# Attention over a small state in front of a two-layer MLP on one core: the second softmax's weights turned by a trip through DRAM and VectorE's 32x32 transposes in place of TensorE, and the first batch's order written anew

## The chip, the cores and the metric

The kernel runs on one core of one Trainium2 chip. The metric is device microseconds of one execution, from start to end. Five engines take part, each with its own queue of instructions: TensorE (PE in the profile; its weight loads are listed apart as PEld), VectorE (DVE), ScalarE (ACT), GpSimd (POOL) and SyncE (SP), which only issues DMAs here.

## The reference

For each of 8 batches and 8 heads, `x` holds 512 tokens of 64 numbers and `state` 32 rows of 64 numbers. Two softmaxes run over the same scores, one over the states, one over the tokens. Their results are put side by side (512 + 32 rows for each batch) and go through a two-layer MLP with 2048 hidden units and a smooth clipped activation.

```
scores  = scale * x @ state^T            # 512 x 32 for each batch and head
a       = softmax(scores, over states)
xread   = a @ state
scores2 = scale * state @ x^T            # 32 x 512
a2      = softmax(scores2, over tokens)  # the second softmax
sread   = a2 @ x
rows    = concat([xread, sread])         # 544 rows for each batch, 8 heads beside each other
h       = rows @ w_in                    # 512 -> 2048
g       = h if h >= 1, 0 if h <= -1, else (h + 1)^2 / 4
out     = g @ w_out                      # 2048 -> 512
```

## The kernel before, in words

**Two algebraic steps shape the work.** `xread` is never formed: `state` is multiplied into `w_in` first (tiles `sw`, line 393, 256 hidden columns to a piece), and the first softmax's weights (`ath` and `atl`, the high and the low part of a value, since each product is made of three reduced-precision ones) go straight against that product (lines 446 to 448, tile `h`). The second product (lines 504 to 506, tile `acc`) is made of three in the same way, from `gh`, `gl` and the two halves of `wo`. `sread` of all batches is collected in `srT` and goes through the MLP at the very end as a ninth, half-sized batch.

**The loop.** Hidden units are taken in eight steps j of 256. In each step of each batch TensorE makes `h` (12 products of 128x512), ScalarE and VectorE make the activation (`relu` L455, `square` L458, `bound` L462) and split it (`gh` L468, `gl` L473), and TensorE multiplies the step before with `w_out` (24 products). The attention of batch b + 1 is spread over the steps of batch b. In step 0 stand its scores (`sc`, L230), the first transposes, the maximum `top2` (L294) and the exponential `exp2` (L298, which also sums). In step 2 stands the rest of the first softmax. The sum over tokens `sread` (`read2`, L327) is made in step 0 of the batch after.

**The turn of the second softmax.** `scores2` lies with (head pair, state) on the 128 partitions and the 512 tokens along the free dimension, in two halves q (even and odd heads). `read2` contracts over tokens, so the exponentials have to lie with tokens on the partitions. `turn2` does that with eight 128x128 TensorE transposes into a PSUM tile `e2p` (L309), and `keep_turned` copies them back to SBUF on ScalarE (L313) and makes the reciprocals of the sums on VectorE (L315, L316).

**What sets the order.** The first batch is issued by hand. Its operations are numbered as they are declared, and the table `ORDER` lists them as words like `186P` (operation 186 on TensorE; S, A and D are SyncE, ScalarE and VectorE). The class `Plan` gives each operation an estimated time, and between TensorE operations that the plan sets apart it emits dummy matmuls (`warmed`, L175), which keep TensorE busy. While the first batch runs, the weights of the MLP are fetched in 16 pieces of 1 MB and turned into fp32: `high` (L558, ScalarE), `low` (L545 on VectorE or L550 on ScalarE, chosen by the table), `join` (L566, VectorE, which makes `w` or `wf`); for `w_out` then two parts (L573 ScalarE, L577 VectorE, tile `wo`). The joined `wf`, the first softmax's `zt` and batch 0's exponentials share two buffers with the tag `tmp`. From batch 1 on a list scheduler orders the instructions.

Of the kernel before, what the change touches and what calls it, by code (L numbers as in the profile page):

```python
# [8 lines left out]
F32 = mybir.dt.float32  # L9
# [3 lines left out]
AF = mybir.ActivationFunctionType  # L13
# [4 lines left out]
WARM = 10  # L18
PAD = 120
ORDER = (  # L20
# [12 lines left out]
)  # L33


class Plan:
# [52 lines left out]
    def emit(self, fill, first, until):  # L89

        self.times(ORDER)
        begun, done = self.begun, self.done
        idle = 0.0
        for k in sorted(begun, key=lambda k: begun[k]):
            if self.ops[k][0] == "PE":
                if begun[first] < begun[k] < begun[until]:
                    n = int((begun[k] - idle) / 0.34)
                    if n > 0:
                        fill(n)
                idle = done[k]  # L100
            run = self.ops[k][2]
            if "/" in self.ops[k][0]:
                run(self.where[k])
            else:
                run()
# [3 lines left out]
def state_exchange_moe(  # L109
# [35 lines left out]
    ps = ctx.enter_context(tc.tile_pool(name="ps", bufs=2, space=PSUM))  # L145
    wop = ctx.enter_context(tc.tile_pool(name="wop", bufs=NJ))
    rawp = ctx.enter_context(tc.tile_pool(name="rawp", bufs=2))

    def ps_acc(name):
        return ps.tile([P, DM], F32, tag="acc", bufs=4, name=name)  # L150
# [10 lines left out]
    def ps_mm(name):  # L161
        return ps.tile([P, 2, 512], F32, tag="mm", bufs=1, name=name)
# [39 lines left out]
    class Attention:  # L202
# [83 lines left out]
        def top2(self, q):  # L286
            b = self.b
            if q == 0:
                tag = "tmp" if b == 0 else "e2"
                self.e2 = work.tile([P, 2, S], F32, tag=tag, bufs=2 if b == 0 else 1, name=f"e2_{b}")  # L290
                self.nm2 = small.tile([P, 2], F32, tag="nm2", name=f"nm2_{b}")
                self.sum2 = small.tile([P, 2], F32, tag="sum2", name=f"sum2_{b}")
            nm = self.nm2[:, q:q + 1]
            nc.vector.tensor_reduce(out=nm, in_=self.sc[q], op=ALU.max, axis=AX.X, negate=True)  # L294
            nc.vector.tensor_scalar_mul(nm, nm, SCALE)

        def exp2(self, q):
            nc.scalar.activation(  # L298
                out=self.e2[:, q], in_=self.sc[q], func=AF.Exp, bias=self.nm2[:, q:q + 1],
                scale=SCALE, accum_out=self.sum2[:, q:q + 1],  # L300
            )

        def turn2(self):
            b, e2 = self.b, self.e2
            e2p = self.e2p = ps_mm(f"e2p{b}")
            for q in range(2):
                for t in range(NT):
                    cols = slice(t * P, (t + 1) * P)
                    nc.tensor.transpose(out=e2p[:, q, cols], in_=e2[:, q, cols], identity=ident)  # L309

        def keep_turned(self):
            b = self.b
            nc.scalar.copy(out=self.e2, in_=self.e2p)  # L313
            self.r2 = small.tile([P, 2], F32, tag="r2", name=f"r2_{b}")
            nc.vector.tensor_scalar_add(self.r2, self.sum2, 1e-9)  # L315
            nc.vector.reciprocal(out=self.r2, in_=self.r2)  # L316

        def read2(self):
            b = self.b
            xn = loaded.pop(("xn", b))  # L320
            sr = banks[1].tile([P, 512], F32, tag="h", name=f"sr{b}") if b else ps_mm(f"sr{b}")[:, 0]
            sr = self.sr = sr[:, :2 * D].rearrange("p (q d) -> p q d", q=2)
            for q in range(2):
                for t in range(NT):
                    for pr in range(NPR):
                        c0 = t * P + pr * NS
                        nc.tensor.matmul(  # L327
                            sr[pr * NS:(pr + 1) * NS, q], lhsT=self.e2[:, q, c0:c0 + NS],
                            rhs=xn[:, t, 2 * pr + q], start=t == 0, stop=t == NT - 1,
                        )  # L330

        def scale2(self):
# [17 lines left out]
        def second(self):  # L350
            for q in range(2):
                self.turn(q)
            for q in range(2):
                self.top2(q)
            for q in range(2):
                self.exp2(q)

        def first(self):
            for f in (self.top1, self.less1, self.exp1, self.sum1):
                for q in range(2):  # L360
                    f(q)
            self.inv1()
            for q in range(2):
                self.norm1(q)
            self.turn2()
            self.keep_turned()

        def halves(self):
            for q in range(2):
# [273 lines left out]
    def att_ops2(b):  # L643
# [3 lines left out]
        for q in range(2):  # L647
# [1 line left out]
            take = [("tmp" if b == 0 else "e2", ("e2", b))] if q == 0 else []  # L649
            op(("top2",) + k, "DVE", 0.8, m("top2", q), [("sc", b) if b else ("sc", b, 1)] + [("top2", b, 0)] * q, take=take)  # L650
            op(("exp2",) + k, "ACT", 0.66, m("exp2", q), [("top2",) + k], ends=[("sc", b)])
        op(("kept", b), "ACT", 0.95, m("keep_turned"), [("e2p", b)], ends=[("e2p", b)])
        if b == 0:
            op(("rs", b), "DVE", 0.25, m("scale2"), [("sr", b)], ends=[("sr", b)])
            op(("srT", b), "ACT", 0.3, m("keep"), [("rt", b)], ends=[("rt", b)])

# [73 lines left out]
    for side in range(2):  # L730
# [12 lines left out]
        2: lambda: tensor(("sc", 1), 1.22, lambda: att_start(1), [("dma", "sb", 1), ("dma", "xt", 1)],  # L743
                          take=[("mm", ("sc", 1))], ends=[("xt", 1)]),
        3: lambda: tensor(("rt", 0), 0.15, lambda: atts[0].keep2(), [("rs", 0)], take=[("mm", ("rt", 0))]),
        4: lambda: tensor(("e2p", 1), 0.92, lambda: atts[1].turn2(), [("exp2", 1, 0), ("exp2", 1, 1)],
                          take=[("mm", ("e2p", 1))]),
    }
    more = {0: [(0, 2)], 1: [(0, 3), (0, 4)], 3: [(0, 5), (0, 6)], 5: [(0, 7), (1, 0)]}
    for j in range(NJ):  # L750
# [84 lines left out]
def _laid_out(x, state, moe_w_in, moe_w_out):  # L835
# [2 lines left out]
    NS = state.shape[2]  # L838
    DM, FF = moe_w_in.shape
    return {  # L840
        "x": x.reshape(B, H, S // 128, 128, D).transpose(0, 3, 2, 1, 4),
        "xt": x.reshape(B, H // 2, 2, 2, S // 2, D).transpose(0, 3, 2, 5, 1, 4).reshape(B, 2, 128, H // 2, S // 2),
        "state": state.reshape(B, H // 2, 2, NS, D).transpose(2, 4, 0, 1, 3).reshape(128, B, H // 2, NS),
        "moe_w_in": moe_w_in.reshape(DM // 128, 128, FF // 256, 256).transpose(2, 1, 0, 3).reshape(FF // 256, 128, -1),
# [27 lines left out]
```

## Time and profile before

| | us |
|---|---|
| median of 3 runs | 654.04 (653.77 to 654.39) |
| the profiled execution | 653.93 |
| its span, first to last instruction | 651.9 |
| TensorE busy in the span | 642.5 |
| ScalarE busy | 362.3 |
| VectorE busy | 338.1 |
| one batch in the middle (two `read2` apart) | 72.5 |

The time of an execution is 2.0 us longer than the span, for what lies around the first and the last instruction. Busy time of TensorE is modelled at the end of each matmul, so two starts that follow each other tell more than a duration: in the middle of the kernel one 128x512 matmul starts 0.23 us after another, though each is listed with 0.39 us.

### The profile page before, as it was taken

The numbers are of one execution on the slowest core, as the hardware profiler recorded it, in microseconds if no ns is written. First come the engines' busy times: TensorE is split into PE (matmuls) and PEld (weight loads), VectorE is DVE, ScalarE is ACT, GpSimd is POOL, SyncE is SP. The second block draws the span as 40 slices with busy tenths as digits, with TensorE's granted clock in tenths as the row PEclk, the third lists the DMA queues.
The fourth block names the chain that finished last, engine by engine and source line by source line (L and its number), as shares of the span: only waits on it lengthen the run. The fifth ranks groups of instructions, "written<-read, shape, count | busy, mean of one in ns | idle before, by whom it ended". The sixth has DMA issues, their size and how long they took to land.

```text
span 651.9 us, 10329 instructions
## 1 busy us (share of the span) xinstructions
PE 642.5 (99%) x4438; PEld 521.2 (80%) x4438; DVE 338.1 (52%) x484; ACT 362.3 (56%) x474; POOL 0.8 (0%) x7
## 2 busy tenths in 40 slices
PE   7999999999999999999999999999999999999997
PEld 6777887878787887878787887878787878788895
DVE  5999958533584338443574339343663334334431
ACT  5999766554565456454664457444664464444632
POOL 0000000000000000000000000000000000000000
PEclk9999999999999999999999999999999999999999
DMA  8996005000400004000500014000300010000101
GB/s 347 387 401 253 1 10 185 0 1 2 168 27 1 1 32 163 0 2 2 193 2 1 1 46 149 1 2 1 130 1 1 0 67 1 0 2 1 64 1 33
DMA packets 11085, 43.64 MB, mean 67 GB/s; under 512 B 1312, under 2 KB 1440, under 8 KB 7968
## 3 DMA queue, kind: packets, MB, share of 16 engines
q1 hardware_dynamic: 6096, 34.28, 13.6%
q10 hardware_dynamic: 4944, 8.72, 3.6%
q8 instruction: 34, 0.56, 0.4%
q14 instruction: 11, 0.09, 0.0%
HBM read 34.08 MB, written 8.91 MB: 66 GB/s over the span
## 4 chain that ended last, share of the span: by engine, by line
PE 96%; DVE 2%; ACT 1%; DMA 0%; issue 0%; POOL 0%; SPq 0%; DVEq 0%; POOLq 0%
PE acc L504 19%; PE acc L505 19%; PE acc L506 19%; PE h L446 10%; PE h L447 10%; PE h L448 10%; PE sw L393 5%; PE sc L230 1%; PE warmed L175 1%; PE sr L327 1%; PE e2p L309 1%; DVE w L566 0%; DVE u L462 0%; DMA out_dram<-o 0%; DVE z L237 0%; DVE z L252 0%
## 5 line engine op out<-in xcount | busy, mean ns | idle before, releaser
L504 PE MATMUL acc<-wo,gh 128*128 128x512 f32 x544 | 214.0, 393 | 0.0
L505 PE MATMUL acc<-wo,gh 128*128 128x512 f32 x544 | 212.1, 390 | 0.0
L506 PE MATMUL acc<-wo,gl 128*128 128x512 f32 x544 | 211.9, 390 | 0.0
L455 ACT ACTIVATE u<-h,half 128x512 f32<-128x512 f32 (+1 forms) x128 | 91.7, 717 | 178.3 <-PE h L448 170.2
L462 DVE SCALAR_TENSOR_TENSOR u<-u,h 128x512 f32<-128x512 f32 (+1 forms) x128 | 86.4, 714 | 199.8 <-ACT u L458 199.6
L504 PEld LDWEIGHTS acc<-wo,gh 128*128 128x128 f32 x544 | 102.2, 188 | 24.4 <-issue 3.3
L506 PEld LDWEIGHTS acc<-wo,gl 128*128 128x128 f32 x544 | 102.1, 188 | 21.6
L505 PEld LDWEIGHTS acc<-wo,gh 128*128 128x128 f32 x544 | 102.2, 188 | 20.6 <-DVE wo L577 0.2
L473 DVE TENSOR_TENSOR gl<-u,gh 128x1024 fp32r<-128x1024 f32 x68 | 83.2, 1224 | 56.5 <-ACT gh L468 56.5
L468 ACT CAST gh<-u 128x1024 fp32r<-128x1024 f32 x68 | 71.5, 1052 | 66.0 <-DVE u L462 63.4
L458 ACT ACTIVATE u<-u 128x1024 f32<-128x1024 f32 x68 | 72.1, 1061 | 1.8
L393 PE MATMUL sw<-w,sb 64*32 64x256 f32 x1024 | 32.3, 380 | 2.5 <-DVE w L566 2.5
L393 PEld LDWEIGHTS sw<-w,sb 64*32 64x32 f32 x1024 | 18.2, 106 | 11.9 <-DVE u L462 2.5
L519 ACT COPY o<-acc 128x512 f32<-128x512 f32 x33 | 19.0, 583 | 12.1 <-PE acc L506 12.1
L446 PE MATMUL h<-ath,sw_3h 128*128 128x512 f32 x64 | 25.1, 393 | 0.0
L446 PE MATMUL h<-ath,sw_5h 128*128 128x512 f32 x64 | 25.0, 391 | 0.0
L447 PE MATMUL h<-ath,sw_5l 128*128 128x512 f32 x64 | 24.9, 389 | 0.0
L448 PE MATMUL h<-atl,sw_5h 128*128 128x512 f32 x64 | 24.9, 389 | 0.0
L447 PE MATMUL h<-ath,sw_3l 128*128 128x512 f32 x64 | 24.9, 389 | 0.0
L448 PE MATMUL h<-atl,sw_3h 128*128 128x512 f32 x64 | 24.9, 389 | 0.0
L446 PE MATMUL h<-ath,sw_1h 128*128 128x512 f32 x60 | 24.4, 407 | 0.5 <-DVE u L462 0.5
L447 PE MATMUL h<-ath,sw_1l 128*128 128x512 f32 x60 | 23.4, 391 | 0.0
(158 smaller groups left out, 722.5 us busy)
## 6 DMA issues: line engine op xcount, KB each, us to landing
xt<-in_xt_dram SPq DMA_DIRECT2D x16, 512.0 KB, 5.2
raw_i<-in_moe_w_in_dram SPq DMA_DIRECT2D x8, 1024.0 KB, 7.0
raw_o<-in_moe_w_out_dram SPq DMA_DIRECT2D x8, 1024.0 KB, 11.4
xn<-in_x_dram SPq DMA_DIRECT2D x8, 1024.0 KB, 6.1
out_dram<-o ACTq DMA_DIRECT2D x32, 256.0 KB, 2.0
sb<-in_state_dram SPq DMA_DIRECT2D x1, 448.0 KB, 8.5
out_dram<-o SPq DMA_DIRECT2D x4, 64.0 KB, 1.7
out_dram<-o ACTq DMA_DIRECT2D x4, 64.0 KB, 2.0
```

What stands on the lines that cost most here:

```text
L393: nc.tensor.matmul(banks[hh][pr * NS:(pr + 1) * NS, cols], lhsT=sb[rows, b, pr], rhs=w32[c][rows, pr], start=True, stop=True,)
L446: nc.tensor.matmul(o, lhsT=wh[:, k, sl], rhs=ah[:, k], start=first, stop=False)
L447: nc.tensor.matmul(o, lhsT=wl[:, k, sl], rhs=ah[:, k], start=False, stop=False)
L448: nc.tensor.matmul(o, lhsT=wh[:, k, sl], rhs=al[:, k], start=False, stop=last)
L455: nc.scalar.activation(out=u, in_=h, func=AF.Relu, scale=0.5, bias=half)
L458: nc.scalar.activation(out=self.u, in_=self.u, func=AF.Square)
L462: nc.vector.scalar_tensor_tensor(out=u, in0=u, scalar=1.0, in1=h, op0=ALU.min, op1=ALU.max)
L468: nc.scalar.copy(out=gh, in_=self.u)
L473: nc.vector.tensor_tensor(out=gl, in0=self.u, in1=gh.bitcast(F32), op=ALU.subtract)
L504: nc.tensor.matmul(a, lhsT=lh, rhs=oh, start=f == 0, stop=False)
L505: nc.tensor.matmul(a, lhsT=lh, rhs=ol, start=False, stop=False)
L506: nc.tensor.matmul(a, lhsT=ll, rhs=oh, start=False, stop=f == NF - 1)
```

## The change

For batches 1 to 7 the turn is made in another way. `exp2` writes the exponentials so that a quarter t of the tokens (128 of them) of both halves q lies together. `trade` writes that tile to DRAM with one DMA (512 KB) and reads it back with four, so that partition block t of 32 holds quarter t for all four head pairs r; that exchanges blocks of 32 partitions with blocks of the free dimension. `turn_traded` then transposes each 32x32 block with one VectorE instruction over 1024 elements of each partition, and makes the reciprocals as before. The eight TensorE transposes and the ScalarE copy of these batches are gone. `read2` takes its weights through a view `turned`, and the host lays `x` out so that the tokens stand on the partitions in the new order (the same 1 MB for each batch).

Batch 0 keeps TensorE's transposes; there `exp2` writes its output in another order of columns, so that the turned tile has the same order of tokens. Its table `ORDER` is another one throughout. Operations are now emitted in the order of the table itself and not sorted by planned start.

```diff
 ORDER = (
-    "0S 87P 86A 1S 2S 88P 6S 97D 90D 89P 91D 99D 92D 10S 93D 100D 94D 3A 98D 101D 95A 33S 102A 96D "
...
+    "86A 0S 87P 1S 88P 2S 3A 90D 97D 91D 98D 89P 99D 92D 100D 93D 101D 10S 4D 6S 94D 102A 95A 5D "
...
+    "175A 176D 238P 239P 179A 234A 235D 236A 180D 237D 85D 59S "
...
-        for k in sorted(begun, key=lambda k: begun[k]):
+        for k in begun:
...
+    dram = ctx.enter_context(tc.tile_pool(name="dram", bufs=2, space=bass.MemoryType.DRAM))
...
         def exp2(self, q):
+            if self.b:
+                o, i = self.e2[:, :, q], self.sc[q].rearrange("p (t k) -> p t k", k=P)
+            else:
+                o = self.e2.rearrange("p t q k -> p (t q k)")
+                o = o[:, q * S:(q + 1) * S].rearrange("p (j t i) -> p t j i", j=NT, i=NS)
+                i = self.sc[q].rearrange("p (t j i) -> p t j i", j=NT, i=NS)
             nc.scalar.activation(
-                out=self.e2[:, q], in_=self.sc[q], func=AF.Exp, bias=self.nm2[:, q:q + 1],
-                scale=SCALE, accum_out=self.sum2[:, q:q + 1],
+                out=o, in_=i, func=AF.Exp,
+                bias=self.nm2[:, q:q + 1], scale=SCALE, accum_out=self.sum2[:, q:q + 1],
             )
...
+        def trade(self):
+            self.e2x = work.tile([P, NPR, 2 * P], F32, tag="tmp", name=f"e2x{self.b}")
+            there = dram.tile([P, NT, 2 * P], F32, tag="e2d", name=f"e2d{self.b}")
+            nc.sync.dma_start(out=there, in_=self.e2.rearrange("p t q k -> p t (q k)"))
+            for t in range(NT):
+                nc.sync.dma_start(
+                    out=self.e2x[t * NS:(t + 1) * NS], in_=there[:, t].rearrange("(r n) k -> n r k", n=NS)
+                )
+
+        def turn_traded(self):
+            e2 = self.e2.rearrange("p t q k -> p (t q k)")
+            nc.vector.transpose(out=e2, in_=self.e2x.rearrange("p r k -> p (r k)"))
+            self.turned = e2.rearrange("p (r q j n) -> p r q j n", q=2, r=NPR, n=NS)
+            self.inv2()
...
         def second(self):
...
             for q in range(2):
                 self.exp2(q)
+            self.trade()
...
         def first(self):
...
-            self.turn2()
-            self.keep_turned()
+            self.turn_traded()
...
-        op(("kept", b), "ACT", 0.95, m("keep_turned"), [("e2p", b)], ends=[("e2p", b)])
-        if b == 0:
+        if b:
+            op(("trade", b), "SP", 6.5, m("trade"), [("exp2", b, 0), ("exp2", b, 1)], take=[("tmp", ("e2x", b))])
+            op(("kept", b), "DVE", 1.3, m("turn_traded"), [("trade", b)], ends=[("e2x", b)])
+        else:
+            op(("kept", b), "ACT", 0.95, m("keep_turned"), [("e2p", b)], ends=[("e2p", b)])
...
-        4: lambda: tensor(("e2p", 1), 0.92, lambda: atts[1].turn2(), [("exp2", 1, 0), ("exp2", 1, 1)],
-                          take=[("mm", ("e2p", 1))]),
```

**What moves, first place: the start of batch 0 on ScalarE and TensorE.** ScalarE before, around the activation of the first hidden step (`u_0` is its tile, `raw_i_200` the third piece of `w_in`, `sw_1` the product of `state` with the second piece):

```order
L407 CAST sw_1h<-sw_1_234 128x2x256
L558 ACTIVATE raw_i_200<-raw_i_200 128x1024
L455 ACTIVATE u_0_220<-h_0_221,half 128x1024
L458 ACTIVATE u_0_220<-u_0_220 128x1024
L298 ACTIVATE e_0_247,sum_0_249<-sc_0_119,nm_0_248 128x512
```

ScalarE in the changed kernel, the same place (the third piece is `raw_i_202` there):

```order
L586 ACTIVATE raw_i_202<-raw_i_202 128x1024
L578 ACTIVATE raw_i_202<-raw_i_202,offset 128x1024
L483 ACTIVATE u_0_227<-h_0_228,half 128x1024
L435 CAST sw_1h<-sw_1_255 128x2x256
L486 ACTIVATE u_0_227<-u_0_227 128x1024
L306 ACTIVATE e_0_233,sum_0_235<-sc_0_119,nm_0_234 128x4x4x32
```

ScalarE now makes both halves of the third piece ahead of the first `relu`, and the cast of `sw_1` has moved from ahead of `relu` to between `relu` and `square`. TensorE before, in the middle of the first hidden step:

```order
L448 MATMUL h_0_221<-atl_118,sw_0h 128x512
L175 MATMUL warmed<-ident 128x128
L393 MATMUL sw_1_234<-w_1_91,sb 32x256 x8
L446 MATMUL h_0_221<-ath_117,sw_0h 128x512
L447 MATMUL h_0_221<-ath_117,sw_0l 128x512
```

TensorE in the changed kernel, from the end of that step on:

```order
L476 MATMUL h_0_228<-atl_118,sw_0h 128x512
L421 MATMUL sw_1_255<-w_1_93,sb 32x256 x8
L177 MATMUL warmed<-ident 128x128 x5
L421 MATMUL sw_2_283<-w_2_94,sb 32x256 x8
L177 MATMUL warmed<-ident 128x128 x2
L474 MATMUL h_1_299<-ath_117,sw_1h 128x512
```

The product `sw_1` stood between the two halves of `h_0` and stands behind all of it now. Ahead of `h_0` there are 14 dummy matmuls where there were 7, and 14 where there were 19 ahead of `sw_0`.

**Second place: the end of batch 0 on VectorE.** Before, from the activation of the last hidden step on (`wo_821` is the last piece of `w_out`):

```order
L462 SCALAR_TENSOR_TENSOR u_7_794<-u_7_794,h_7_795 128x1024
L577 TENSOR_TENSOR wo_821<-wf_803,wo_821 128x1024
L282 TENSOR_TENSOR atl_467<-zt_823,ath_466 128x512 x2
L315 TENSOR_SCALAR r_1_875<-sum_1_497 128x2
L316 RECIPROCAL r_1_875<-r_1_875 128x2
L473 TENSOR_TENSOR gl_7_871<-u_7_794,gh_7_870 128x1024
```

In the changed kernel (the last piece of `w_out` is `wo_840`):

```order
L490 SCALAR_TENSOR_TENSOR u_7_794<-u_7_794,h_7_795 128x1024
L284 TENSOR_TENSOR atl_476<-zt_837,ath_475 128x512
L501 TENSOR_TENSOR gl_7_872<-u_7_794,gh_7_871 128x1024
L605 TENSOR_TENSOR wo_840<-wf_811,wo_840 128x1024
L490 SCALAR_TENSOR_TENSOR u_0_887<-u_0_887,h_0_0_888 128x512
```

The last part of `w_out` now comes behind `gl` of the last step instead of ahead of it, as VectorE's last work of the batch.

**Third place: a batch in the middle, on VectorE and SyncE.** VectorE in the changed kernel, from the activation of step 2 to that of step 3 (before, nothing stood between `gl` and the activation of step 3):

```order
L284 TENSOR_TENSOR atl_912<-zt_1315,ath_911 128x512 x2
L501 TENSOR_TENSOR gl_2_1140<-u_2_1119,gh_2_1139 128x1024
L337 STREAM_TRANSPOSE e_2_1048<-e2x_1057 128x1024
L490 SCALAR_TENSOR_TENSOR u_3_1183<-u_3_1183,h_3_0_1184 128x512
L490 SCALAR_TENSOR_TENSOR u_3_1183<-u_3_1183,h_3_1_1185 128x512
```

SyncE in the changed kernel, for one batch and the beginning of the next:

```order
L201 DMA xn_1036<-in_x_dram 128x2048
L196 DMA xt_1033<-in_xt_dram 128x1024 x2
L329 DMA e2d_1058<-e_2_1048 128x1024
L331 DMA e2x_1057<-e2d_1058 32x4x256 x4
L201 DMA xn_1624<-in_x_dram 128x2048
```

The new transpose stands behind `gl` of step 2, and the five new DMAs stand behind the batch's three loads, with the next batch's first load behind them. On TensorE nothing else differs in these batches than the eight transposes that are gone.

More of the change, by code (lines that the diff above doesn't have):

```diff
@@ L289, in top2 @@
                 tag = "tmp" if b == 0 else "e2"
-                self.e2 = work.tile([P, 2, S], F32, tag=tag, bufs=2 if b == 0 else 1, name=f"e2_{b}")
+                self.e2 = work.tile([P, NT, 2, P], F32, tag=tag, bufs=2 if b == 0 else 1, name=f"e2_{b}")
                 self.nm2 = small.tile([P, 2], F32, tag="nm2", name=f"nm2_{b}")
@@ L305, in turn2, with inv2 @@
             e2p = self.e2p = ps_mm(f"e2p{b}")
+            e2 = e2.rearrange("p t q k -> p (t q k)")
             for q in range(2):
-                for t in range(NT):
-                    cols = slice(t * P, (t + 1) * P)
-                    nc.tensor.transpose(out=e2p[:, q, cols], in_=e2[:, q, cols], identity=ident)
+                for j in range(NT):
+                    c = (q * NT + j) * P
+                    nc.tensor.transpose(out=e2p[:, q, j * P:(j + 1) * P], in_=e2[:, c:c + P], identity=ident)
         def keep_turned(self):
+            e2 = self.e2.rearrange("p t q k -> p (t q k)")
+            nc.scalar.copy(out=e2, in_=self.e2p.rearrange("p q s -> p (q s)"))
+            self.turned = e2.rearrange("p (q j r n) -> p r q j n", q=2, r=NPR, n=NS)
+            self.inv2()
[8 more added lines that the diff above has]
+        def turn_traded(self):
+            e2 = self.e2.rearrange("p t q k -> p (t q k)")
+            nc.vector.transpose(out=e2, in_=self.e2x.rearrange("p r k -> p (r k)"))
+            self.turned = e2.rearrange("p (r q j n) -> p r q j n", q=2, r=NPR, n=NS)
+            self.inv2()
+        def inv2(self):
             b = self.b
-            nc.scalar.copy(out=self.e2, in_=self.e2p)
             self.r2 = small.tile([P, 2], F32, tag="r2", name=f"r2_{b}")
@@ L323, in read2 @@
             for q in range(2):
-                for t in range(NT):
+                for j in range(NT):
                     for pr in range(NPR):
-                        c0 = t * P + pr * NS
                         nc.tensor.matmul(
-                            sr[pr * NS:(pr + 1) * NS, q], lhsT=self.e2[:, q, c0:c0 + NS],
-                            rhs=xn[:, t, 2 * pr + q], start=t == 0, stop=t == NT - 1,
+                            sr[pr * NS:(pr + 1) * NS, q], lhsT=self.turned[:, pr, q, j],
+                            rhs=xn[:, j, 2 * pr + q], start=j == 0, stop=j == NT - 1,
                         )
@@ L840, in _laid_out @@
     return {
-        "x": x.reshape(B, H, S // 128, 128, D).transpose(0, 3, 2, 1, 4),
+        "x": x.reshape(B, H, 4, S // 128, 32, D).transpose(0, 2, 4, 3, 1, 5).reshape(B, 128, S // 128, H, D),
         "xt": x.reshape(B, H // 2, 2, 2, S // 2, D).transpose(0, 3, 2, 5, 1, 4).reshape(B, 2, 128, H // 2, S // 2),
```

21 rows, old and new, of the table ORDER are left out of this document.

## The prediction

> **What bounds the kernel now.** I read the page first, then a table by stage, then the chain of waits in order of time, then TensorE's timeline around the instructions that go.
>
> ```profile
> PE 642.5 (99%) x4438; PEld 521.2 (80%) x4438; DVE 338.1 (52%) x484; ACT 362.3 (56%) x474; POOL 0.8 (0%) x7
> PE   7999999999999999999999999999999999999997
> PE 96%; DVE 2%; ACT 1%; DMA 0%; issue 0%; POOL 0%; SPq 0%; DVEq 0%; POOLq 0%
> ```
>
> TensorE is busy in every slice but the first and the last, and 96% of the chain that ended last is its own. The stages say where it isn't full (columns: window, length, then busy us of PE, PEld, DVE, ACT, POOL, the granted clock, the DMA share and GB/s):
>
> ```profile
> 10.00:20.00 10.00, 8.00 (x72) 6.75 (x71) 9.76 (x16) 9.34 (x11) 0.00 (x0) 0.83 0.99 395
> 40.00:50.00 10.00, 10.00 (x56) 7.37 (x55) 9.88 (x13) 9.96 (x10) 0.00 (x0) 1.00 0.98 387
> 172.10:244.60 72.50, 72.50 (x510) 58.42 (x513) 35.42 (x55) 38.59 (x53) 0.00 (x0) 1.00 0.12 44
> ```
>
> A batch in the middle is 72.5 us of TensorE without a hole, while VectorE and ScalarE are half idle and the DMA engines at 0.12. At the start TensorE has holes; until 50 us VectorE, ScalarE and the DMAs are full. So two questions decide: what TensorE no longer does, and when its unbroken work begins.
>
> **What goes: seven passes of eight transposes.** The chain lists each pass of `e2p`:
>
> ```profile
> 81.04 0.87 PE e2p L309 x8
> ...
> 480.56 0.87 PE e2p L309 x8
> ```
>
> Eight passes are in the trace; the one of batch 0 stays, the seven from 81.04 to 480.56 go. All stand in the chain at 0.87 us. The starts beside the pass of 190 us agree (start, us, instruction):
>
> ```profile
> 190.17 0.39 PE L506 MATMUL acc<-wo,gl 128*128 128x512 f32 x1
> 190.40 1.03 PE L309 MATMUL e2p<-ident,e 128*128 128x128 f32 x8
> 191.19 0.48 PE L504 MATMUL acc<-wo,gh 128*128 128x512 f32 x1
> 191.51 0.39 PE L505 MATMUL acc<-wo,gh 128*128 128x512 f32 x1
> ```
>
> From 190.17 two ordinary matmuls would have brought L505 to 190.17 + 2 x 0.23 = 190.63; it started at 191.51, 0.88 later. So 7 x 0.87 = 6.09 us leave the path, and since no engine feeds TensorE at those places, nothing takes their room. The group view would tempt to another price:
>
> ```profile
> L309 PE MATMUL e2p<-ident,e 128*128 128x128 f32 x64 | 8.3, 272 | 0.0
> L276 DVE STREAM_TRANSPOSE zt<-z 128x512 f32<-128x512 f32 x16 | 10.6, 694 | 0.1
> L298 ACT ACTIVATE e<-sc,nm 128x512 f32<-128x512 f32 x16 | 10.9, 684 | 1.7 <-DVE nm L295 1.7
> L346 ACT COPY srT<-rt 128x128 f32<-128x128 f32 x8 | 2.1, 259 | 0.5 <-PE rt L341 0.5
> ```
>
> 56 transposes at the listed 272 ns would be 15.2 us, but they overlap: eight start within 0.79 us. [...]
>
> **What comes on VectorE.** One transpose of 1024 elements for each of seven batches. Two of 512 at 694 ns bound it from above by 1.39 us, one of 512 from below by 0.69; I take 1.3. Its place in a middle batch is behind `gl` of step 2:
>
> ```profile
> 191.50 1.23 DVE L473 TENSOR_TENSOR gl<-u,gh 128x1024 fp32r<-128x1024 f32 x1
> 198.08 1.28 DVE L462 SCALAR_TENSOR_TENSOR u<-u,h 128x512 f32<-128x512 f32 x2 [5.36 <-ACT u L458]
> 200.54 1.23 DVE L473 TENSOR_TENSOR gl<-u,gh 128x1024 fp32r<-128x1024 f32 x1 [1.17 <-ACT gh L468]
> ```
>
> VectorE idles 5.36 us there, so 1.3 us and the two small reciprocal operations (they exist already and move along) cost nothing. If that cover goes, the activation of step 3 at 198.08 is what gets late.
>
> **What the transpose waits for: the trade.** It starts when the second `exp2` has ended:
>
> ```profile
> 181.10 0.20 ACT L298 ACTIVATION_READ_ACCUMULATOR e<-sc,nm 128x1 f32 x1
> 201.51 0.39 PE L446 MATMUL h<-ath,sw_3h 128*128 128x512 f32 x1
> 204.23 0.39 PE L504 MATMUL acc<-wo,gh 128*128 128x512 f32 x1
> 176.00 0.82 SPq L194 DMA_DIRECT2D xt<-in_xt_dram  x2
> xt<-in_xt_dram SPq DMA_DIRECT2D x16, 512.0 KB, 5.2
> raw_o<-in_moe_w_out_dram SPq DMA_DIRECT2D x8, 1024.0 KB, 11.4
> out_dram<-o ACTq DMA_DIRECT2D x32, 256.0 KB, 2.0
> sb<-in_state_dram ACTq DMA_DIRECT2D x1, 64.0 KB, 3.9
> ```
>
> A write of 512 KB, then four reads of 128 KB, each issued in 0.41 us (0.82 for two). No run here shows such a trip. From below: two landings like the store's 2.0 us and four issues, 2.0 + 1.6 + 2.0 = 5.6. From above: the slowest median landing, then the issues and a 512 KB load, 11.4 + 1.6 + 5.2 = 18.2. I take 8, near the lower end, for those long landings were taken behind other transfers at a DMA share near 1, and here it is 0.12. Then the tile lies there at 181.3 + 8 = 189.3, before VectorE has ended `gl` at 192.7. It may come as late as 198.08 - 1.6 = 196.5 before step 3's activation is late at all, and TensorE first feels that when it needs `gl` of step 3, which ends at 201.77, at 204.23: 2.4 us more, 198.9, or 17.6 us after `exp2`. On SyncE only the next batch's load waits behind the five DMAs, 50 us off. In the first batch the load of `xn` for batch 1 is put behind the trade, 30 us ahead of its use.
>
> **What else moves off the path.** ScalarE loses seven copies of 1 us, hidden before, so nothing is gained in the middle batches. `exp2` writes in runs of 512 bytes (128 in batch 0). The nearest row, L346, writes runs of 32 elements and takes 259 ns for 128; L298 takes 684 for 512. Both ends of that price, 0 and about 0.3 us in each batch, lie in ScalarE's idle time; I take 0. The PSUM tile of the transposes falls away as well.
>
> **The start of batch 0.** TensorE's unbroken work begins at 25.46, with `h_1`:
>
> ```profile
> 7.50 4.51 PE L175 MATMUL warmed<-ident 128*128 128x128 f32 x38
> 14.01 0.67 PE L393 MATMUL sw<-w,sb 64*32 64x256 f32 x16 [2.00 <-DVE w L566]
> 14.61 3.30 PE L175 MATMUL warmed<-ident 128*128 128x128 f32 x14
> 21.46 0.40 PE L448 MATMUL h<-atl,sw_0h 128*128 128x512 f32 x1
> 25.46 0.50 PE L446 MATMUL h<-ath,sw_1h 128*128 128x512 f32 x1 [0.45 <-DVE u L462]
> 18.72 0.68 DVE L282 TENSOR_TENSOR atl<-zt,ath 128x512 fp32r<-128x512 f32 x1
> 20.84 0.70 DVE L545 TENSOR_SCALAR raw_i<-raw_i 128x1024 int32<-128x1024 uint32 x1 [0.65 <-DMA raw_i<-in_moe_w_in_dram]
> 21.96 1.10 ACT L455 ACTIVATE u<-h,half 128x1024 f32<-128x1024 f32 x1
> 23.10 1.06 ACT L458 ACTIVATE u<-u 128x1024 f32<-128x1024 f32 x1
> ```
>
> Before: `atl` ends at 19.40, then `sw_1` and half of `h_0` run until 21.86, `relu` starts at 21.96, and `h_1` 3.50 later. After: `sw_1` stands behind `h_0`, so `h_0` ends about 0.7 sooner, near 21.1. But ScalarE now makes both halves of the third `w_in` piece first. Half of that was VectorE's, at 20.84, once the piece had landed as the sixth megabyte. It comes as the fifth and a half now and is asked for some 2 us sooner, so it may land at 18.7 to 19.4; with two operations of 1.1 us `relu` starts at 20.9 to 21.6. The cast of `sw_1` between `relu` and `square` adds 0.5, so `h_1` starts 4.0 later, at 24.9 to 25.6. Against 25.46 that is -0.6 to +0.1; I take -0.3.
>
> From there ScalarE loses a copy and VectorE gains a transpose in a stage where both are full; it ends here:
>
> ```profile
> 89.77 1.22 DVE L473 TENSOR_TENSOR gl<-u,gh 128x1024 fp32r<-128x1024 f32 x1
> 94.02 0.39 PE L504 MATMUL acc<-wo,gh 128*128 128x512 f32 x1
> ```
>
> VectorE ended its last part for step 7 at 90.99, and TensorE took it at 94.02, 3.0 us of room. The last `wo` part (1.2 us) now comes behind `gl`, the transpose adds up to 1.6, and TensorE comes 0.9 sooner. That is 0.7 over, against which the batch's first activations have no fixed time; I price it 0 to 0.7 and take 0, because step 7's `gl` follows TensorE's own `h_7`.
>
> **Sum.** 653.93 - 6.09 - 0.30 = 647.54 against the profiled execution. The median lies 0.11 above that execution, so 647.6.
>
> **Rivals.**
> - The start loses. TensorE waited 2.0 us before 14.01, and the 14 rows after 14.61 took 0.24 us each, where the 38 before took 0.12: the clock was at a half (0.83 in the mean of that stage). After, 14 dummies end near 10.8 and 14 more near 16.1, which leaves two gaps of about 1.4 us. If the second brings the half clock, it hits `h_0`'s twelve matmuls, and not dummies: 0.23 us more for each that it hits, and for three to eight of them 0.7 to 1.8, 648.3 to 649.4. [...] A gap of 1.4 is shorter than the one that did it, so 0.18.
> - The start gains more, since less ScalarE work lies in its way: `h_1` at 24.3, 646.7, chance 0.08.
> - VectorE is late at the end of batch 0, by the 0.7 above or somewhat more: 648.4, chance 0.04.
> - The transposes cost what their durations say: 638.4, chance 0.01; the starts speak against it.
> - The new table costs nearly what the passes bring, 4.8 to 7.4 us, from pieces of weights that come late: 654, chance 0.02. Against it: the DMAs bring the same megabytes, in another order.
> - Slower: the trip through DRAM is late. From 17.6 us after `exp2` on, each further microsecond costs one in each of six batches; from 18.9 us on (6 x 1.3 eats 6.4 and 1.3) the kernel is slower, and at 20 us it ends near 662. For it: the trip has runs of 1 KB, and the row with small runs, `sb`, needed 3.9 us for only 64 KB. Against it: `sb` went out as the run began, and my upper bound of 18.2 does not get there. Chance 0.05. The trade working but its transposes coming after `read2` wants them is excluded by 50 us.
>
> **How the numbers follow.** 0.62 for 647.6, with the start between -0.8 and +0.5 (646.9 to 648.3). The range 646.6 to 649.4 takes in the half clock, the late `gl` and half of the larger gain: about 0.87. A change of 0.2% (1.3 us) is about what a measurement of this kernel can tell from none. Faster: 0.62 + 0.18 + 0.08 + 0.04 + 0.01 = 0.93; within it 0.02; slower 0.05.
>
> **What would show it.** Right: a middle batch takes 71.6 us instead of 72.5; `acc` follows `acc` where `e2p` stood; VectorE waits for no DMA ahead of the new transpose, which takes 1.2 to 1.4 us; `h_1` starts at 24.9 to 25.6; `read2` of batch 1 starts 1.2 us sooner. Wrong: VectorE idle released by the DMA of the traded tile; a clock under 1.00 between 17 and 22 us; TensorE idle between 26 and 100 us.

## The result, and the profile after

The changed kernel takes 648.25 us in the median (648.05 to 648.89, 4 runs), the kernel before 653.98 (653.77 to 654.39) beside it: a ratio of 0.9913, 95% interval 0.9896 to 0.9931. The profiled execution took 648.17, 0.08 under its median, with a span of 646.4. It lies 0.6 above the forecast of 647.6 and inside its range. That small distance hides a gain and a loss in the first batch, which the experiments take apart.

The page of the changed kernel, its engines, TensorE's slices and the chain's shares:

```profile
PE 635.7 (98%) x4382; PEld 513.6 (79%) x4382; DVE 346.4 (54%) x492; ACT 354.1 (55%) x466; POOL 0.8 (0%) x7
PE   8999999999999999999999999999999999999997
PE 92%; DVE 4%; DMA 2%; ACT 1%; issue 0%; SPq 0%; POOL 0%; POOLq 0%
```

TensorE has 56 instructions and 6.8 us of busy time less. But its share of the chain of waits that ended last fell from 96% to 92%: VectorE (4% instead of 2%) and a DMA (2% instead of 0) hold a stretch of the path that TensorE held before. The stages say where (the columns are those of the prediction's table):

```profile
40.00:50.00 10.00, 10.00 (x57) 7.70 (x42) 7.73 (x11) 9.32 (x11) 0.00 (x0) 1.00 0.97 402
50.00:60.00 10.00, 8.52 (x65) 6.14 (x63) 10.00 (x12) 6.96 (x8) 0.00 (x0) 1.00 0.71 233
171.50:243.20 71.70, 71.70 (x512) 57.69 (x515) 36.64 (x56) 37.67 (x53) 0.00 (x0) 1.00 0.17 60
```

The middle batch has no hole, and from one `read2` to the next it takes 71.59 us instead of 72.50. Between 50 and 60 us, however, TensorE is busy for 8.52 of 10. VectorE is busy all through that stage, and for only 7.73 us in the one before: it was held up there and pays for it afterwards.

**The bookkeeping.** Starts of `read2` split the difference of 5.76 us between the two profiled executions (653.93 and 648.17):

| stretch | before | after | difference |
|---|---|---|---|
| start to `h_1` | 25.46 | 24.27 | -1.19 |
| `h_1` to `read2` of batch 1 | 74.09 | 75.53 | +1.44 |
| `read2` of batch 1 to that of the last batch's tokens (six batches) | 362.50 + 74.39 | 357.97 + 73.48 | -5.44 |
| from there to the last instruction | 115.45 | 115.13 | -0.32 |
| outside the span | 2.04 | 1.79 | -0.25 |

The six batches behind the first give all that they should. The first batch, which holds the seventh pass and the earlier start, should have given 1.19 + 0.88. Instead `read2` of batch 1 starts 0.25 later (-1.19 + 1.44): the batch lost what it had won. The last two rows are no effect of the change. From the last row's `read2` to the last matmul both profiles take the same, 110.49 and 110.51 us; the 0.32 lies in the last store behind it. The experiments' profiles have 114.9 to 115.2 there, the one that turns batches 2 to 7 by TensorE too, and what lies outside the span went from 1.76 to 2.56 us in runs of the kernel before alone.

**The hole.** TensorE's timeline of the changed kernel at 51 us (start, us, instruction, and in brackets the idle time ahead of it and what ended it):

```profile
51.50 0.39 PE L534 MATMUL acc<-wo,gl 128*128 128x512 f32 x1
53.36 0.50 PE L474 MATMUL h<-ath,sw_3h 128*128 128x512 f32 x1 [1.48 <-DVE u L490]
```

TensorE waits 1.48 us for `bound` of step 3 (tile `u`). VectorE's timeline of the changed kernel shows why that is late, and ScalarE's below it what VectorE waited for:

```profile
45.90 0.68 DVE L296 TENSOR_REDUCE nm<-sc 128x1 f32<-128x512 f32 x1
48.97 0.69 DVE L296 TENSOR_REDUCE nm<-sc 128x1 f32<-128x512 f32 x1 [2.20 <-ACT e L306]
52.10 1.21 DVE L490 SCALAR_TENSOR_TENSOR u<-u,h 128x1024 f32<-128x1024 f32 x1
...
48.16 0.68 ACT L306 ACTIVATE e<-sc,nm 128x512 f32<-128x512 f32 x1
```

The second maximum `top2` of batch 1 stands still for 2.20 us, until the first `exp2` has ended. It needs nothing of it. Both only read the scores `sc`, the one for the odd heads, the other for the even ones. In the kernel before the same place reads:

```profile
42.22 0.68 DVE L294 TENSOR_REDUCE nm<-sc 128x1 f32<-128x512 f32 x1
48.92 0.65 DVE L294 TENSOR_REDUCE nm<-sc 128x1 f32<-128x512 f32 x1
50.27 1.21 DVE L462 SCALAR_TENSOR_TENSOR u<-u,h 128x1024 f32<-128x1024 f32 x1
...
50.24 0.68 ACT L298 ACTIVATE e<-sc,nm 128x512 f32<-128x512 f32 x1
```

No brackets: both maxima were over before the first `exp2` began. In the new table the word of that `exp2` stands between the two words of the maxima (`181D 182A 183D`), and operations are now written in the table's order. The reading of the trace is that an instruction on VectorE that is written behind a reader of the same PSUM tile on another engine is given a wait for it. That is a hypothesis until the words are moved.

Earlier on TensorE there are two smaller holes, of 0.17 us at 35.08 and of 0.47 at 39.68. The chain leads from them to VectorE once more, which waited for a piece of `w_out` there:

```profile
34.13 0.70 DVE L573 TENSOR_SCALAR raw_o<-raw_o 128x1024 int32<-128x1024 uint32 x1 [1.21 <-DMA raw_o<-in_moe_w_out_dram]
```

A second profile of the same kernel (experiment 9) has neither this wait nor these two holes, and 74.86 us from `h_1` to `read2` of batch 1 instead of 75.53. So about 0.65 us of the +1.44 above belong to this one execution.

**The trade.** SyncE, ScalarE and VectorE of the changed kernel in the middle batch:

```profile
180.67 0.33 SPq L329 DMA_DIRECT2D e2d<-e  x1
183.34 1.75 SPq L331 DMA_DIRECT2D e2x<-e2d  x4
...
179.88 0.68 ACT L306 ACTIVATE e<-sc,nm 128x512 f32<-128x512 f32 x1
180.45 0.20 ACT L306 ACTIVATION_READ_ACCUMULATOR e<-sc,nm 128x1 f32 x1
...
190.84 1.23 DVE L501 TENSOR_TENSOR gl<-u,gh 128x1024 fp32r<-128x1024 f32 x1
191.98 1.24 DVE L337 STREAM_TRANSPOSE e<-e2x 128x1024 f32<-128x1024 f32 x1
196.52 1.28 DVE L490 SCALAR_TENSOR_TENSOR u<-u,h 128x512 f32<-128x512 f32 x2 [3.30 <-ACT u L486]
```

The page's list of DMA issues (tile, count, size of each, median us from issue to landing):

```profile
e2d<-e SPq DMA_DIRECT2D x7, 512.0 KB, 2.6
e2x<-e2d SPq DMA_DIRECT2D x28, 128.0 KB, 2.8
```

`exp2` ends at 180.65, the write lands 2.6 us after its issue, the last read at 187.56 (issue 184.66): 6.9 us for the trip. VectorE takes the tile at 191.98 without a wait and still has 3.30 us idle behind it. `exp2` takes 0.68 us as before.

### The profile page after: what moved, and what is told of

It is laid out like the page before. It is cut to its first block, busy times and chain, and to the rows that moved or that the text cites. A ratio compares the mean times of both kernels' runs of the same rounds, so it can differ in the third digit from the quotient of the medians.

```text
span 646.4 us, 10270 instructions
## 1 busy us (share of the span) xinstructions
PE 635.7 (98%) x4382; PEld 513.6 (79%) x4382; DVE 346.4 (54%) x492; ACT 354.1 (55%) x466; POOL 0.8 (0%) x7
## 4 chain that ended last, share of the span: by engine, by line
PE 92%; DVE 4%; DMA 2%; ACT 1%; issue 0%; SPq 0%; POOL 0%; POOLq 0%
PE acc L532 19%; PE acc L533 18%; PE acc L534 18%; PE h L474 10%; PE h L475 10%; PE h L476 10%; PE sw L421 4%; DMA raw_o<-in_moe_w_out_dram 2%; PE sr L355 1%; PE sc L232 1%; PE warmed L177 1%; DVE wf L594 1%; DVE w L594 1%; DVE u L490 1%; DMA out_dram<-o 0%
## 5 line engine op out<-in xcount | busy, mean ns | idle before, releaser
L534 PEld LDWEIGHTS acc<-wo,gl 128*128 128x128 f32 x544 | 102.1, 188 | 21.6
L421 PEld LDWEIGHTS sw<-w,sb 64*32 64x32 f32 x1024 | 18.2, 106 | 11.9 <-DVE u L490 2.5
L475 PE MATMUL h<-ath,sw_5l 128*128 128x512 f32 x64 | 24.9, 390 | 0.0
L475 PE MATMUL h<-ath,sw_3l 128*128 128x512 f32 x64 | 24.9, 390 | 0.0
L476 PE MATMUL h<-atl,sw_5h 128*128 128x512 f32 x64 | 24.9, 389 | 0.0
L476 PE MATMUL h<-atl,sw_3h 128*128 128x512 f32 x64 | 24.9, 389 | 0.0
```

The source lines that it names most:

```text
L421: nc.tensor.matmul(banks[hh][pr * NS:(pr + 1) * NS, cols], lhsT=sb[rows, b, pr], rhs=w32[c][rows, pr], start=True, stop=True,)
L475: nc.tensor.matmul(o, lhsT=wl[:, k, sl], rhs=ah[:, k], start=False, stop=False)
L476: nc.tensor.matmul(o, lhsT=wh[:, k, sl], rhs=al[:, k], start=False, stop=last)
L534: nc.tensor.matmul(a, lhsT=ll, rhs=oh, start=False, stop=f == NF - 1)
```

## The experiments

The edits are to the changed kernel unless said otherwise. Each ratio is to the kernel before on the same chip, where it had medians of 654.26 (experiments 1 to 4), 654.39 (5 to 8) and 654.38 (9 to 11). Beside these experiments the changed kernel itself ran on the last chip alone; in experiments 1 to 8 a distance from its 648.25 us may be one between chips, and the ratios, 0.9913 for it, are the safer measure.

**1. The maxima ahead of `exp2`.**

```diff
-    "... 53S 181D 182A 183D 62D 191A 167D 46D 184A ..."
+    "... 53S 181D 183D 62D 167D 182A 191A 46D 184A ..."
```

> The changed kernel with one edit: in the table of the first batch the words for the second maximum (`top2`, half 1) and for the second half's turn of batch 1 stand ahead of the word for the first `exp2` of batch 1. Each engine keeps its own order of instructions; only the order in which they are written changes, and with it VectorE's wait on ScalarE. Theory A (that wait makes the 1.48 us hole in TensorE at 51.5 us and eats the gain of the start): the 2.2 us wait of `top2` on `exp2` is gone, `bound` of step 3 ends some 1.5 us sooner, the hole is gone, and the time falls by 1.3 to 1.7 us against the changed kernel, to 646.6 to 647.0. Theory B (weights set the pace up to 60 us, so that another wait takes its place): the hole moves to a later step, and the time falls by 0.5 us or less.

Measured: 646.59 us (646.13 to 647.53), ratio 0.9884 (0.9869 to 0.9899). VectorE, ScalarE and TensorE of this kernel at the same place:

```profile
45.51 0.68 DVE L296 TENSOR_REDUCE nm<-sc 128x1 f32<-128x512 f32 x1
46.29 0.68 DVE L296 TENSOR_REDUCE nm<-sc 128x1 f32<-128x512 f32 x1
50.19 1.22 DVE L490 SCALAR_TENSOR_TENSOR u<-u,h 128x1024 f32<-128x1024 f32 x1 [0.69 <-ACT u L486]
...
48.42 0.69 ACT L306 ACTIVATE e<-sc,nm 128x512 f32<-128x512 f32 x1 [0.45 <-DVE z L239]
...
50.97 0.39 PE L534 MATMUL acc<-wo,gl 128*128 128x512 f32 x1
51.46 0.50 PE L474 MATMUL h<-ath,sw_3h 128*128 128x512 f32 x1
```

The wait is gone, `bound` comes 1.91 us sooner, and TensorE's hole has shrunk from 1.86 between two starts to 0.49. ScalarE's first `exp2` now stands 0.45 us for VectorE's second turn, and `bound` 0.69 us for ScalarE, but no hole on TensorE comes of it: theory A. `read2` of batch 1 starts 73.24 us after `h_1`, against 74.09 in the kernel before and 75.53 after: the 0.85 less than before is about the pass of batch 1 that the change was to save.

**2. The new first batch alone.** `exp2` and `trade` take the new form for batch 1 only; the batches behind are turned by TensorE.

```diff
-            if self.b:
+            if self.b == 1:
...
-            self.trade()
...
-            self.turn_traded()
+            self.turn2()
+            self.keep_turned()
```

> The changed kernel with the new first batch (table, order of writing, batch 1 traded through DRAM), but batches 2 to 7 turned by TensorE again. Theory A (the new first batch brings nothing net: h_1 1.19 us sooner and one pass of 0.87 less, both lost again by 53 us): within 0.4 us of the kernel before, 653.7 to 654.3. Theory B (what batch 1's pass cost is gained at least): 0.8 us or more faster than before, 653.2 or less.

Measured: 653.77 us (652.78 to 654.64, 11 runs) against 654.26, ratio 0.9990 (0.9982 to 0.9999). That is 0.5 us under the kernel before, and not 0.8 or more: theory A by its time (653.7 to 654.3), though the distance is a little over its 0.4. The 2.3 us wait of `top2` on `exp2` is in this profile too, and TensorE's hole ahead of `h_3` is 1.70 us.

**3. The steady batches alone.** The kernel before up to batch 1 (table, order of writing, TensorE's turn), the trade from batch 2 on. The lines of the old table and of batch 1's turn are left out here.

```diff
...
-            if self.b:
+            if self.b > 1:
...
-        for k in begun:
+        for k in sorted(begun, key=lambda k: begun[k]):
...
```

> The kernel before in the first batch (its table, its order of writing, batches 0 and 1 turned by TensorE), and the trade through DRAM for batches 2 to 7 alone. Theory A (six passes of 0.91 us leave the path, and that is the whole of the change): 653.98 - 5.46 = 648.5, 648.2 to 648.8. Theory B (the new first batch is worth the 0.9 us of batch 1's pass): 0.9 us behind the changed kernel, 649.1 or more.

Measured: 648.23 us (647.93 to 648.39), ratio 0.9904 (0.9891 to 0.9918). That is the changed kernel's time without any of its new first batch: theory A. Nearly the whole gain of the change, in time, comes from six of its seven passes; experiment 2 leaves 0.5 us for the rest.

**4. The new table, written in the old order.**

```diff
-        for k in begun:
+        for k in sorted(begun, key=lambda k: begun[k]):
```

> The changed kernel, but its first batch's operations are written in the order of their planned start again, as before, and not in the order of the table's words. The table is the new one. `top2` of batch 1 then stands ahead of `exp2` once more, while the second half's turn still stands behind it. Theory A (the wait between two readers of the scores is what is lost): part of the hole at 51.5 us goes, 0.4 to 1.4 us faster than the changed kernel. Theory B (weights set the pace): within 0.3 us of the changed kernel.

Measured: 646.91 us (646.32 to 648.00), ratio 0.9887 (0.9873 to 0.9900): 1.3 us under the changed kernel (1.7 by the ratios), at theory A's upper end or a little above. The maxima are written ahead of `exp2` again, the second half's turn of the scores is not, and it is there that VectorE now waits:

```profile
46.77 0.68 DVE L296 TENSOR_REDUCE nm<-sc 128x1 f32<-128x512 f32 x1
49.14 0.72 DVE L239 STREAM_TRANSPOSE z<-sc 128x512 f32<-128x512 f32 x1 [0.89 <-ACT e L306]
50.88 1.21 DVE L490 SCALAR_TENSOR_TENSOR u<-u,h 128x1024 f32<-128x1024 f32 x1
```

TensorE's idle time ahead of `h_3` is 0.31 us in this profile. In these runs the wait followed whichever VectorE reader of `sc` was written behind `exp2`: 2.20 us for the maximum in the changed kernel, 0.89 for the turn here. Another explanation of the changed kernel's wait would be the tile `nm`: `top2` writes one column of it, and the first `exp2` reads the other. The turn that waits here writes only `z`, so it shares nothing but `sc` with `exp2`. It also goes the other way: in the changed kernel ScalarE's second `exp2` stood 1.22 us, until 51.11, for VectorE's turn written ahead of it. The edit also changes where a few loads stand in SyncE's queue and one instruction in VectorE's, so this run alone would not settle it; with the first it does. Whether the chip could do without such a wait, no run here shows: the experiments only move it.

**5 and 6. A longer trip.** Between the write and the reads the tile is copied two (six) more times from DRAM to DRAM, in batches 2 to 7.

```diff
             nc.sync.dma_start(out=there, in_=self.e2.rearrange("p t q k -> p t (q k)"))
+            for _ in range(2 if self.b > 1 else 0):   # 6 in the second kernel
+                further = dram.tile([P, NT, 2 * P], F32, tag="hop", name="hop")
+                nc.sync.dma_start(out=further, in_=there)
+                there = further
```

> The changed kernel, but in batches 2 to 7 the traded tile is copied twice more from DRAM to DRAM (512 KB each, one after another) before the four reads, so that it lands later. In the changed kernel it lands 7 us after the second `exp2` of a middle batch. Theory A (TensorE feels the trip only from 17.6 us after `exp2` on): with two copies at 2.5 to 4 us each it lands 12 to 15 us after `exp2`; VectorE may wait for it, the time stays within 0.4 us of the changed kernel (648.25). Theory B (the trade has little room; the wait that it gives to VectorE is handed on at once): 3 us or more slower than the changed kernel (0.5 us or more for each of six batches).

> The same with six more copies from DRAM to DRAM in batches 2 to 7. Landing is expected 22 to 30 us after `exp2`. Theory A: from 17.6 us on each microsecond costs one in each of six batches, so 26 to 74 us slower than the changed kernel, 674 to 722, with VectorE's idle time released by the DMA of the traded tile and TensorE idle behind step 3 of each batch. Theory B (the list scheduler or spare buffers take up the delay): under 10 us slower.

Measured: 647.92 us (647.15 to 649.64) and 647.57 us (647.40 to 648.77), ratios 0.9903 (0.9887 to 0.9920) and 0.9900 (0.9884 to 0.9917). Neither is slower: for two copies theory A. With six copies the tile is there at 211.05, 30.9 us after `exp2`, and the price of 26 to 74 us that theory A set on that does not appear. SyncE and VectorE of that kernel:

```profile
180.17 0.33 SPq L329 DMA_DIRECT2D e2d<-e  x1
182.76 0.48 SPq L332 DMA_DIRECT2D hop<-e2d  x1
186.71 16.18 SPq L332 DMA_DIRECT2D hop<-hop  x5
206.39 1.76 SPq L335 DMA_DIRECT2D e2x<-hop  x4
...
208.97 1.22 DVE L441 TENSOR_TENSOR sw_7l<-sw,sw_7h 128x1024 fp32r<-128x1024 f32 x1
211.24 1.25 DVE L341 STREAM_TRANSPOSE e<-e2x 128x1024 f32<-128x1024 f32 x1 [1.05 <-DMA e2x<-hop]
```

The transpose no longer stands behind `gl` of step 2. It stands after step 4, and VectorE waits there 1.05 us in each of six batches, in time that it has: the six batches take 431.45 us, as in the changed kernel. With two copies the tile lands at 195.00, 15.1 us after `exp2`, and the transpose stands at 196.97, behind `bound` of step 3, without a wait. The order from batch 1 on is a scheduler's, and the scheduler moved the reader along with the trip. Theory B of the second kernel.

**7. No dummy matmuls** between the planned operations of the first batch.

```diff
-                        fill(n)
+                        fill(0)
```

> The changed kernel without the dummy matmuls between the planned operations of the first batch (those at the very beginning stay). TensorE then idles some 4.5 and 3.8 us ahead of `sw_0` and of `h_0`. Theory A (such idle time brings the half clock, as 2.0 us did before; but TensorE's start is not what holds the first batch, VectorE's wait at 51.5 us is): a clock under 1.00 during `h_0`, `h_1` 2 to 2.8 us later, and a total only 0 to 0.8 us above the changed kernel. Theory B (what the start loses goes through to the end): 2 to 2.8 us above it, 650.3 to 651. Theory C (no half clock): `h_1` within 0.3 us of the changed kernel's 24.3.

Measured: 651.78 us (651.63 to 652.31), ratio 0.9960 (0.9945 to 0.9975). That is 3.5 us above the changed kernel (3.1 by the ratios): theory B, and somewhat more. TensorE's timeline of this kernel, and below it two of its stages:

```profile
13.05 1.11 PE L421 MATMUL sw<-w,sb 64*32 64x256 f32 x16 [4.49 <-DVE w L594]
17.44 0.79 PE L474 MATMUL h<-ath,sw_0h 128*128 128x512 f32 x1 [3.29 <-ACT ath L281]
```

```profile
18.00:22.00 4.00, 4.00 (x10) 2.77 (x9) 3.97 (x6) 3.30 (x4) 0.00 (x0) 0.50 1.00 424
26.00:32.00 6.00, 5.18 (x32) 3.98 (x18) 5.86 (x8) 4.55 (x8) 0.00 (x0) 0.72 0.96 366
```

`h_0` ran at a granted clock of 0.50, 0.43 us from one start to the next instead of 0.23; `h_1` started at 27.08, and from 26 to 32 us the granted clock was 0.72. And the hole ahead of `h_3` was still there, 2.09 us between two starts (1.86 in the changed kernel), from 55.03 on. So it is no fixed date that a late start could hide in: VectorE's chain starts from TensorE's `h`, and the wait came on top of the late start.

**8. The same with the maxima ahead of `exp2`.**

> Without the dummy matmuls, as in the run before, and with the second maximum and turn of batch 1 written ahead of the first `exp2` (as in the experiment of that kind, 646.59). There the hole at 51.5 us is gone, so the start should count. Theory A: `h_1` 2 to 2.8 us later than 24.6, and most of it is in the total: 1.5 to 2.8 us above 646.59, 648.1 to 649.4. Theory B (weights or VectorE hold the first batch anyway, wherever TensorE starts): within 0.5 us of 646.59.

Measured: 650.30 us (649.11 to 650.76), ratio 0.9933 (0.9918 to 0.9948), 3.7 us above the first experiment (3.2 by the ratios). `h_1` started at 26.32, and the granted clock was 0.50 from 18 to 22 us and again from 26 to 32. Theory A in kind, and again more than its figure, for it left out the half clock in `h_1` itself: with the 0.43 us instead of 0.23 of the seventh run's `h_0`, an estimate of 12 x 0.2 = 2.4 us.

**9 and 10. The changed kernel and the one of the first experiment again**, side by side, with no new edit.

> The changed kernel once more, beside the version with early maxima, both on one chip. Theory (the wait between the two readers of the scores costs 1.5 to 2 us of every execution): the changed kernel is 1.3 to 2 us slower than that version. Rival (the earlier difference lay between chips): within 0.5 us of each other.

> The version with the second maximum and turn of batch 1 written ahead of its first `exp2`, as before. Theory: 1.3 to 2 us faster than the changed kernel on the same chip, so a ratio to the kernel before of 0.988 to 0.989 where the changed kernel has 0.991. Rival: the same ratio for both.

Measured: 648.29 us (647.94 to 649.02), ratio 0.9910 (0.9895 to 0.9924), and 646.91 us (646.18 to 648.62), ratio 0.9892 (0.9874 to 0.9910). The intervals overlap, but all eight runs of each together have means of 648.37 and 646.93, 1.44 apart, and only one of the eight lies above the lowest of the other kernel. On this chip alone the medians are 1.38 apart, at the theory's lower end. Theory. This version and that of experiment 4 (646.91) are the fastest that were run.

**11. A longer trip where the order is fixed.** Six more copies in batch 1 alone.

```diff
+            for _ in range(6 if self.b == 1 else 0):
```

> The changed kernel with six more copies from DRAM to DRAM in batch 1 alone, whose instructions stand in the order written by hand, so that the transpose keeps its place behind the activation of step 6 (78.82 us; the tile lands at 70.86). With 3.9 us for each copy the tile lands at 89 to 91 us. Theory A (a trip is late where the place of its reader is fixed; in the batches that the list scheduler orders it moves the reader and loses nothing): VectorE waits 9 to 12 us for the DMA of the traded tile, TensorE idles 7 to 10 us of it ahead of step 7's products, and the time is 7 to 10 us above the changed kernel, 655 to 658. Theory B (VectorE's room takes it up here too): less than 2 us slower.

Measured: 659.80 us (658.20 to 662.67), ratio 1.0089 (1.0062 to 1.0116): 11.5 us above the changed kernel on that chip, slower than the kernel before. VectorE and TensorE in the timeline, and below them the stage behind:

```profile
91.89 1.25 DVE L341 STREAM_TRANSPOSE e<-e2x 128x1024 f32<-128x1024 f32 x1 [11.14 <-DMA e2x<-hop]
...
96.29 0.79 PE L537 MATMUL acc<-wo,gh 128*128 128x512 f32 x1 [5.71 <-DVE wo L609]
```

```profile
95.00:100.00 5.00, 3.37 (x7) 2.38 (x8) 4.93 (x9) 2.22 (x3) 0.00 (x0) 0.50 0.33 134
```

The tile landed at 91.77, and VectorE waited 11.14 us for it, as forecast. TensorE's longest idle time is 5.71 us and not 7 to 10, and behind it TensorE ran at half clock until about 100, as in the seventh run. Not all of the 11.5 us is the trip's. In this profile `h_1` of batch 0 ran at half clock too, at 25 us, long before the copies (the last section comes back to that), and `h_3` started at 55.27, 2.15 later than in experiment 9. Of the 12.3 us between these two profiles that leaves 10.1 behind `h_3`. Theory A, at the upper end of its price: the same trip that costs nothing in six scheduled batches costs about 10 us in the one whose order is written by hand.

## Why the prediction was right, and where it was not

- **Seven passes of 0.87 us: right for six of them.** A middle batch lost 0.91 us (71.59), 5.44 for six where 5.22 was in the sum. "Nothing takes their room" held there. For batch 1 it failed: the 0.87 was saved, as experiment 1 shows, and spent again in the same batch.
- **The start: the term was mis-sized on its good side.** Forecast -0.30, measured -1.19; the rival with `h_1` at 24.3 came about (24.27). The third piece of `w_in` landed at 18.2, sooner than the 18.7 to 19.4 of the working, so `relu` began at 20.44 instead of 20.9 to 21.6. Part of that is the one execution: `h_1` started between 24.20 and 25.45 in the nine profiles with the new table and its dummies, at 24.73 in the mean, and in three of them inside the forecast's 24.9 to 25.6. Times say the same. Experiment 1, which has the new first batch without the wait, is 1.64 us faster than experiment 3, which has the old one, on one chip; 0.85 of that is the pass, which leaves 0.8 for the start.
- **The step that failed: the order of writing was priced at nothing.** The prediction followed batch 0 from its start to its end on each engine, priced what lies between at 0 to 0.7 and took 0; it did not look at the waits that come from the order in which instructions are written across engines. That wait is the missing term. From `h_1` to `read2` of batch 1 four profiles with the wait (experiments 2, 5, 6 and 9) take 74.83 to 74.87 us, two without it 73.24 and 73.26, so it costs 1.6 us; the profile with 75.53 holds the late piece of `w_out` besides. By time it is 1.44. The forecast of `read2` 1.2 us sooner was wrong for this: it came 0.25 later. The prediction's own sign of error, "TensorE idle between 26 and 100 us", is what showed it.
- **That the sum came out near is partly luck.** The profiled execution lost 5.76 us where 6.39 were forecast. The 0.63 between them are errors of both signs: -0.9 at the start, +2.3 from `h_1` to `read2` of batch 1 (forecast -0.87, measured +1.44: 1.6 for the wait and 0.65 for the late piece), -0.2 in the six batches, and -0.6 in the last store and outside the span, which the change has no part in.
- **The trade: right.** Trip 6.9 us instead of 8, transpose 1.24 us instead of 1.3, no wait of VectorE on a DMA, `exp2` no longer than before.
- **The rival of the late trip: its price was wrong.** "From 17.6 us after `exp2` on, each further microsecond costs one in each of six batches" supposed that the reader stays where it stands. At 30.9 us it cost nothing, since the scheduler moved it. A limit showed where the order is fixed, in batch 1 alone (landing at 91.77 in experiment 11, 11.14 us of wait on VectorE).
- **The end of batch 0: right,** nothing was lost there; VectorE ended its last `wo` at 93.7.
- **Half clock in `h_0`: did not come in the changed kernel's profile** (1.00 throughout; idle 1.17 us ahead of `sw_0`, 0.41 and 0.38 in `h_0`). Experiment 7 shows it behind idle times of 4.49 and 3.29 us (granted clock 0.50 from 14 to 22 us) and, by the starts, its price in `h_0`: 0.43 us for a matmul instead of 0.23.

## What to carry to other kernels

When work is taken off a path, look at the order in which instructions are written as closely as at each engine's own order: a reader of a shared tile that was written behind another engine's reader waited 2.20 us for it here though it needs nothing of it, and two words in a table were worth 1.4 us, more than the better start. A term that is banked must be followed to the next point at which both kernels can be compared (here `read2` of batch 1), for a gain at 25 us can be gone by 53. How late a transfer could be depended here on who places its reader: a scheduler moved it along at no cost (six copies in batches 2 to 7, 647.57 us), a written order paid about 10 us (the same six in batch 1 alone, 659.80).

## What the runs showed of the hardware that was not expected

**Idle times of TensorE of nearly one length, 2.00 and 1.99 us, were followed by a granted clock of 0.50 in one profile and of 1.00 in another.** Experiment 3 has the kernel before's order on TensorE at the start, and the same wait as the 2.00 us that the prediction quotes at 14.01:

```profile
15.09 0.67 PE L421 MATMUL sw<-w,sb 64*32 64x256 f32 x16 [1.99 <-DVE w L594]
15.69 1.49 PE L177 MATMUL warmed<-ident 128*128 128x128 f32 x11
```

There the 14 rows of dummies behind it took 0.24 us each, and the clock was 0.59 from 14 to 18 us. Here the eleven rows that the view lists took 0.14 each, and the clock was 1.00 from 12 to 20 us. It differs within one kernel too: of the 15 executions of the kernel before beside experiments 1 to 4, eight have a mean clock of 0.996 or 0.997 and seven of 0.999 or 1.000, at the same times (means of 654.25 and 654.33 us). Where in them the clock was lower, no profile shows; in the one profile it is the row of dummies that was hit (0.50 from 15 to 18 us). In experiment 11, whose first 50 us are the changed kernel's, an idle time of 1.77 us at 22 us (0.81 in the changed kernel) was followed by `h_1` at half clock (0.50 from 26 to 28 us):

```profile
23.97 0.67 PE L425 MATMUL sw<-w,sb 64*32 64x256 f32 x16 [1.77 <-DVE sw_1l L441]
24.56 0.79 PE L177 MATMUL warmed<-ident 128*128 128x128 f32 x4
25.45 0.79 PE L478 MATMUL h<-ath,sw_1h 128*128 128x512 f32 x1
26.05 0.63 PE L479 MATMUL h<-ath,sw_1l 128*128 128x512 f32 x1
```

So idle times of 2.00 and 1.77 us were followed by the half clock, and one of 1.99 us in another execution was not. What made the difference, no run here shows.

**A copy of 512 KB from DRAM to DRAM took 3.9 us to land** in experiment 6 (median, at a DMA share of 0.30 from 171.0 to 242.6 us), 2.6 for the write from SBUF; the six copies in a row, from the issue of the first at 182.76 to the landing of the last at 206.34, took 23.6.
